# Block-sparse attention and a feed-forward net in one kernel: the first segment scored in fp32 from the raw rows, the mask built in five operations a part, weight lows that scale as they subtract, and new ranks in the planner

## The chip, the cores and the metric

The kernel runs on one core of one Trainium2 chip. The metric is the device time of one execution in microseconds, the median of several runs. Profiles come from one execution each; all times in a profile are counted from the first instruction.

## The reference

```python
# attention: B, H, S, D = 4, 8, 768, 64; blocks of 32; scale = 1/8
scores = scale * q @ k.T
mask = |blk_i - blk_j| <= 1, or row or column block first or last, or blk_j in sampled_blocks[blk_i]  # 3 a row
scores = where(mask, scores, -1e9);  attn = softmax(scores);  a = attn @ v
# feed-forward on x = a laid out as (4, 768, 512)
xn = (x - mean) / sqrt(var + 1e-6) * g_ln
out = x + relu(xn @ w_ch1) @ w_ch2        # 512 -> 2048 -> 512
```

q, k and v come in fp32. The two weight matrices come in 64 bits a number, and the kernel makes fp32 of their bits itself.

## The kernel before

**Work.** A unit is one batch and 256 query rows: 12 units. A unit has four segments, one for each pair of heads, and a segment has two query tiles of 128 rows, so four slots (tile, head). A pair of heads shares one 128-row tile of q and k, each head in 64 of its rows. Precision comes from splitting: a number x is kept as a half-precision high part and the rest as a half-precision low part, and a product is three half-precision matmuls (high by high, high by low, low by high).

**A slot.** TensorE (PE) writes the scores of both heads of a tile (`scores`, line 518, "ps"); VectorE (DVE) adds the mask and takes the maximum in one custom operation (`masked_max`, line 527); ScalarE (ACT) takes the exponential with the sum (`exponent`, line 541). Then there are two ways. The first `EARLY` segments go the early way: PE transposes the fp32 probabilities (line 556), ACT copies them out of PSUM (line 563, "pt"), and PE multiplies them with v in fp32 (line 632) and spreads the sums (line 657). All others go the usual way: ACT and DVE write the scaled high and low (lines 593 and 597, "ph" and "pl"), the DMA queue transposes them, and PE multiplies in half precision (lines 636 and 641). Before a v tile of an early segment is used the usual way later, ACT scales it (line 373) and splits it.

**After a unit's four segments** come the layer norm and the feed-forward net. For the first `EARLYLN` units the mean and the variance are fp32 matmuls against ones (line 713), for the others DVE adds four parts to one first and PE needs two half-precision matmuls for each (lines 705 and 706). The first product, here "up", is 192 matmuls (line 800), whose bank ACT and DVE turn into `hh` and `hl` (lines 815 and 821), and the second, "down", is 192 matmuls (line 860 for unit 0, which takes the weight rows in order; line 881 for the others).

**Weights.** Eight parts of w1 (each 1 MB of raw bits) and 16 of w2 (0.5 MB) are loaded and converted while the first units run. DVE shifts and masks the bits in three operations (lines 465, 469, 473), ACT scales (line 500), ACT writes the high (line 502), and GpSimd (POOL), or for parts named in `LOWDVE` DVE, writes the low (line 504). For parts in `PORC` the third operation is a short one (line 478) and POOL adds (line 483), so that ACT has no scaling to do.

**Start.** The first k and q ("raw" and "qr") are loaded first; ACT casts the high of k (line 335), DVE the high of q (line 356), and DVE subtracts both lows (lines 362 and 330). `build_mask` then makes the mask of the first two tiles in eight DVE operations (lines 288 to 298), and that of the other four in as many, later.

**Order.** `Plan` holds every task with an engine, a cost, a rank and what it waits for; it plays the program through once and emits the tasks in the order that comes out. Each engine then works in that order and waits at each instruction for what it needs: a later one never overtakes. DMAs are issued by SP's queue in order as well. Ranks come from the tables (`W1AT`, `W2AT`, `KAT`, `MASKAT` and so on).

## Time and profile before

| | |
|---|---|
| median of three runs | 797.96 us (797.42 to 801.64) |
| the profiled execution | 798.02 us, of which its span is 796.2 us |
| PE busy | 768.0 us, 96% of the span |
| DVE, ACT, POOL busy | 610.5, 519.1, 156.2 us |
| granted TensorE clock | 1.00 |
| first scores, first up, first down matmul | 5.01, 80.66, 124.94 us |
| last matmul ends | 792.85 us |

The table says which engine is busy over the whole span, not what holds it up at a given time: the stages have to be taken apart. A bracket behind a row of the timeline gives how long that engine sat idle before it, and what released it.

### The profile page before, as it was taken

The page shows a single profiled execution, that of the slowest core. Times are in us where ns is not written, and L with a number is a line of the kernel's source. Part 1 is how long each engine was busy: PE and PEld are TensorE (multiplying, and loading weights), DVE is VectorE, ACT ScalarE, POOL GpSimd, SP SyncE. Part 2 cuts the span into 40 slices and gives each one's busy share as a digit, 9 for nine tenths or more (in the row PEclk, how much of TensorE's full clock was granted, in tenths as well). Part 3 has the DMA queues.
Part 4 walks back from the last instruction along what each step waited for, and adds up shares of the span by engine and source line. Part 5 has one row for each costly group of instructions (what it writes and reads, how often), then busy time and mean ns, then how long its engine had stood idle before and what let it go on. Part 6 is the DMA issues. An engine that isn't in the chain of part 4 may idle for free.

```text
span 796.2 us, 18337 instructions
## 1 busy us (share of the span) xinstructions
PE 768.0 (96%) x7208; PEld 588.2 (74%) x7208; DVE 610.5 (77%) x1193; ACT 519.1 (65%) x974; POOL 156.2 (20%) x171
## 2 busy tenths in 40 slices
PE   5879899999999999999999999999999999999998
PEld 2555567777877777877777877677777777788887
DVE  6999999978887887877887978778978789744020
ACT  5899988868776666677666766668767667613010
POOL 2564423342110112322211013231110100000000
PEclk9999999999999999999999999999999999999999
DMA  8653459998887779897978789799887886620000
GB/s 313 204 199 119 122 102 218 199 198 158 150 129 153 132 140 175 163 185 145 162 132 133 148 152 162 157 189 168 151 147 130 132 138 122 110 62 2 28 1 28
DMA packets 298342, 112.61 MB, mean 141 GB/s; under 512 B 266640, under 2 KB 290064, under 8 KB 298256
## 3 DMA queue, kind: packets, MB, share of 16 engines
q1 hardware_dynamic: 290192, 106.49, 66.2%
q0 software_dynamic: 7776, 4.85, 5.1%
q8 instruction: 57, 0.93, 0.5%
q14 instruction: 29, 0.24, 0.1%
q10 hardware_dynamic: 288, 0.10, 0.1%
HBM read 45.46 MB, written 6.29 MB: 65 GB/s over the span
## 4 chain that ended last, share of the span: by engine, by line
PE 85%; DVE 8%; ACT 3%; DMA 2%; issue 1%; SPq 0%; DVEq 0%
PE bank L800 29%; PE bank L881 27%; PE ps L518 11%; PE pa L636 7%; PE pa L641 3%; PE bank L860 3%; DVE p L527 2%; PE pa L632 2%; ACT p L541 1%; PE bank L556 1%; ACT pt L563 1%; DVE w2l L504 1%; DVE pl L597 1%; DMA pt<-pl 1%; DMA raw<-w 1%
## 5 line engine op out<-in xcount | busy, mean ns | idle before, releaser
L881 PE MATMUL bank<-hh,w2h 128*128 128x256 f16 x704 | 192.2, 273 | 0.0
L881 PE MATMUL bank<-hh,w2l 128*128 128x256 f16 x704 | 191.9, 273 | 0.0
L881 PE MATMUL bank<-hl,w2h 128*128 128x256 f16 x704 | 191.9, 273 | 0.0
L527 DVE CUSTOM_DVE_ANT_1 p<-ps,allow 128x768 f32<-128x768 f32 x192 | 178.2, 948 | 12.5 <-PE ps L518 12.2
L541 ACT ACTIVATE p<-p,st 128x768 f32<-128x768 f32 x192 | 178.1, 930 | 14.1 <-DVE st L527 14.0
L597 DVE SCALAR_TENSOR_TENSOR pl<-p,st,ph 128x768 f16<-128x768 f32 x164 | 167.0, 1036 | 24.2 <-DMA pt<-pl 22.3
L593 ACT ACTIVATE ph<-p,st 128x768 f16<-128x768 f32 x164 | 148.9, 928 | 43.8 <-DVE st L584 26.7
L800 PEld LDWEIGHTS <-w1h 128*128 128x128 f16 x1536 | 147.4, 98 | 30.5 <-issue 13.8
L881 PEld LDWEIGHTS <-w2h 128*128 128x128 f16 x1408 | 135.0, 98 | 24.1 <-issue 8.8
L800 PE MATMUL bank<-xh,w1h 128*128 128x256 f16 x768 | 115.4, 273 | 4.4 <-ACT pt L563 2.3
L815 ACT ACTIVATE hh<-bank 128x512 f16<-128x512 f32 x96 | 56.9, 592 | 91.2 <-PE bank L800 90.7
L800 PE MATMUL bank<-xl,w1h 128*128 128x256 f16 x768 | 115.4, 273 | 0.0
L800 PE MATMUL bank<-xh,w1l 128*128 128x256 f16 x768 | 115.3, 273 | 0.0
L821 DVE SCALAR_TENSOR_TENSOR hl<-bank,hh 128x512 f16<-128x512 f32 x96 | 66.0, 688 | 48.4 <-ACT hh L815 47.7
L636 PE MATMUL pa<-pt,vh 128*64 128x512 f16 x492 | 83.3, 383 | 0.0
L800 PEld LDWEIGHTS <-w1l 128*128 128x128 f16 x768 | 74.3, 98 | 11.0 <-issue 2.6
L518 PE MATMUL ps<-kh,qh 64*128 64x256 f16 (+1 forms) x384 | 69.1, 332 | 11.7 <-DVE st L527 6.7
L881 PEld LDWEIGHTS <-w2l 128*128 128x128 f16 x704 | 68.9, 98 | 8.0
L518 PEld LDWEIGHTS <-qh 64*128 64x128 f16 x768 | 31.9, 95 | 57.5 <-issue 28.9
L641 PE MATMUL pa<-pt,vl 128*64 128x256 f16 x492 | 67.9, 273 | 0.0
L518 PE MATMUL ps<-kl,qh 64*128 64x256 f16 (+1 forms) x384 | 66.9, 327 | 0.7 <-DVE kl L330 0.7
L518 PE MATMUL ps<-kh,ql 64*128 64x256 f16 (+1 forms) x384 | 65.8, 327 | 0.0
(114 smaller groups left out, 897.3 us busy)
## 6 DMA issues: line engine op xcount, KB each, us to landing
raw<-k SPq DMA_DIRECT2D x16, 384.0 KB, 4.8
qr<-q SPq DMA_DIRECT2D x48, 128.0 KB, 3.7
raw<-w SPq DMA_DIRECT2D x12, 512.0 KB, 4.4
out<-ot SPq DMA_DIRECT2D x48, 128.0 KB, 1.9
vr<-v SPq DMA_DIRECT2D x24, 192.0 KB, 2.9
w2l<-w SPq DMA_DIRECT2D x4, 1024.0 KB, 8.6
qh<-q POOLq DMA_DIRECT2D x44, 64.0 KB, 3.6
pt<-ph SPq DMA_TRANSPOSE x164, 2.8
```

The source lines that it names most:

```text
L518: nc.tensor.matmul(s.ps[:, lo:hi], x[rows, s.qs], y[rows, lo:hi], start=n == 0, stop=n == len(terms) - 1)
L527: nc.vector.tensor_tensor_reduce(out=s.p.rearrange(blk, k=BLK), in0=s.ps[:, 0:S].rearrange(blk, k=BLK), in1=bias, scale=-0.125, scalar=3.0 ...
L541: nc.scalar.activation(s.p, s.p, AF.Exp, bias=s.st[:, j : j + 1], scale=-1.0, accum_out=total)
L593: nc.scalar.activation(s.ph, s.p, AF.Copy, scale=s.r)
L597: nc.vector.scalar_tensor_tensor(out=s.pl, in0=s.p, scalar=s.r, in1=s.ph, op0=ALU.mult, op1=ALU.subtract)
L636: nc.tensor.matmul(seg.pa[half[hh], 0 : 2 * CH], vo.vh[:, hh, t, :], pts[keys[hh]][:, t].rearrange("p i n -> p (i n)"), start=t == 0, stop ...
L641: nc.tensor.matmul(seg.pa[half[hh], 0:CH], vo.vl[:, hh, t, :], pts[keys[hh]][:, t, 0, :], start=False, stop=t == KT - 1, skip_group_check= ...
L800: nc.tensor.matmul(dst, w[:, ct, fs], x[:, ct, :], start=n == 0 and ct == 0, stop=n == 2 and ct == CT - 1, skip_group_check=True)
L815: nc.scalar.activation(u.hh[:, f : f + 2, :].rearrange("p f n -> p (f n)"), bank[plan.where("bank", own)], AF.Relu)
L821: nc.vector.scalar_tensor_tensor(out=u.hl[:, f : f + 2, :].rearrange("p f n -> p (f n)"), in0=bank[plan.where("bank", own)], scalar=0.0, i ...
L860: nc.tensor.matmul(dst(e), w[:, f, e * P : (e + 1) * P], x[:, f, :], start=f == 0 and n == 0 and e % 2 == 0, stop=f == FT - 1 and n == 2, ...
L881: nc.tensor.matmul(dst, w[:, k, e * P : (e + 1) * P], x[:, k, :], start=k == 0 and n == 0, stop=k == FT - 1 and n == 2)
```

## The change

It has four parts and new numbers for the planner.

1. The first segment (`RAWS_S = 1`) is scored by one fp32 matmul a part from the raw k and q rows, in place of three half-precision ones. The high and the low of the first q are no longer made; those of the first k still are, since later units need them, its low now on POOL. The raw buffer of the first k comes free when both the low and the segment's last score are done.
2. `build_mask` compares all three sampled blocks at once, straight from the integers, and then takes three maxima and one affine operation.
3. Parts in `LOWDVE` and not in `PORC` skip ACT's scaling: ACT writes the high with the scale, and DVE writes the low as scale times source minus high in one operation.
4. `EARLY` goes from 7 to 8, so that all of units 0 and 1 go the early way, and `EARLYLN` from 2 to 1, so that unit 1's layer norm goes the usual way.
5. New tables; `LOWDVE` holds one part of w1 and eight of w2 (before: one and twelve), `PORC` two of w1 and five of w2 (before: one and five).

```diff
-    LOOK = 60
+    LOOK = 90
...
-    EARLY = 7
-    EARLYLN = 2
-    EASY, EASE = 34, (34, 1649, 802)
-    PORC = ((1, 6), (2, 1), (2, 5), (2, 12), (2, 15), (2, 0))
+    EARLY = 8
+    EARLYLN = 1
+    EASY, EASE = 50, (210, 1787, 613)
+    PORC = ((1, 6), (2, 1), (2, 5), (1, 0), (2, 4), (2, 14), (2, 0))
...
+    RAWS_S = 1
+    SPLITAT = -2.2
+    LOWDVE = ((2, 0), (2, 6), (2, 7), (2, 12), (2, 1), (2, 11), (2, 8), (1, 0), (2, 14))
...
-    W2AT = (15.45, 15.53, 15.97, 18.44, 18.44, 18.89, 21.76, ...
+    W2AT = (10.58, 12.15, 16.02, 16.59, 18.19, 19.41, 20.61, ...
...
-        nc.vector.tensor_copy(samp_f[:, ts],
-                              samp_i.rearrange("p c (r t) -> p c r t", t=2)[:, ts, :, 0])
...
+        hit = one[:, 0 : n * NR * NB].rearrange("p (t r n) -> p t r n", r=NR, n=NB)
+        ids = allow[:, KT : KT + 1, :].unsqueeze(1).to_broadcast([P, n, NR, NB])
+        got = samp_i.rearrange("p c (r t) -> p c r t", t=2)[:, ts, :, 0:1]
+        nc.vector.tensor_tensor(out=hit, in0=ids, in1=got.to_broadcast([P, n, NR, NB]),
+                                op=ALU.is_equal)
         for r in range(NR):
-            nc.vector.tensor_tensor(out=hit, in0=ids,
-                                    in1=samp_f[:, ts, r : r + 1].to_broadcast([P, n, NB]),
-                                    op=ALU.is_equal)
-            nc.vector.tensor_tensor(out=allow[:, ts], in0=allow[:, ts], in1=hit, op=ALU.max)
+            nc.vector.tensor_tensor(out=allow[:, ts], in0=allow[:, ts], in1=hit[:, :, r],
+                                    op=ALU.max)
...
+            d = c if own in LOWDVE else plan.add(
+                "ACT", 960 * size + 60, lambda: nc.scalar.activation(
+                    o.src, o.src, AF.Copy, scale=scale), (c,), rank)
+        left = scale if own in LOWDVE and own not in PORC else 1.0
...
+                nc.scalar.activation(o.dh, o.src, AF.Copy, scale=left)
...
+                nc.vector.scalar_tensor_tensor(out=o.dl, in0=o.src, scalar=left, in1=o.dh,
+                                               op0=ALU.mult, op1=ALU.subtract)
...
-        terms = (q.qh, k.kh), (q.qh, k.kl), (q.ql, k.kh)
+        terms = ((q.qr, k.kr),) if a.seg.i < RAWS_S else (
+            (q.qh, k.kh), (q.qh, k.kl), (q.ql, k.kh))
```

The order of the engines' queues shows what the new ranks do. First DVE at the start of the program, from its first instruction on data, before and then after the change ("w1h<-allow" and "allow" are the mask, "p,st<-ps,allow" the masked maximum, "w2h<-w1r" a weight part's bits, "w1l" a weight low).

```order
L356 CAST qh_132<-qr_133 128x256
L362 TENSOR_TENSOR ql_121<-qr_133,qh_132 128x256
L330 TENSOR_TENSOR kl_130<-raw_119,kh_129 128x768
...
L527 ISA p_190,st_191<-ps_169,allow 128x768
...
L527 ISA p_197,st_191<-ps_170,allow 128x768
...
L465 TENSOR_SCALAR w2h<-w1r_156 128x1024
L469 SCALAR_TENSOR_TENSOR w2h<-w1r_156,w2h 128x1024
L527 ISA p_224,st_225<-ps_203,allow 128x768
...
L473 SCALAR_TENSOR_TENSOR w2h<-w1r_156,w2h 128x1024
```

```order
L293 TENSOR_TENSOR w1h<-allow,samp_i 128x144
L296 TENSOR_TENSOR allow<-allow,w1h 128x48 x3
L298 TENSOR_SCALAR allow<-allow 128x48
L546 ISA p_176,st_177<-ps_152,allow 128x768
...
L546 ISA p_179,st_177<-ps_153,allow 128x768
...
L468 TENSOR_SCALAR w2h<-w1r_150 128x1024
L472 SCALAR_TENSOR_TENSOR w2h<-w1r_150,w2h 128x1024
L481 TENSOR_SCALAR w1r_150<-w1r_150 128x1024
L546 ISA p_203,st_204<-ps_186,allow 128x768
```

The three operations on q and k are gone from the head of the queue; behind the first two maxima all three bit operations of the first weight part now stand ahead of the next maximum, where before two did.

Then DVE around the end of unit 0's up product, where the last `hl` stands; line 716 and its neighbours are unit 1's layer norm, "xc" its centring, "raw" a w2 part's bits, "w2l" a w2 low. Before the change:

```order
L821 SCALAR_TENSOR_TENSOR hl_1075<-bank_102,hh_1068 128x512
L597 SCALAR_TENSOR_TENSOR pl_1470<-p_1307,st_1308,ph_1418 128x768
L597 SCALAR_TENSOR_TENSOR pl_1491<-p_1322,st_1308,ph_1438 128x768
L821 SCALAR_TENSOR_TENSOR hl_1075<-bank_103,hh_1068 128x512
L504 TENSOR_TENSOR w2l<-raw_120,w2h 128x512
L465 TENSOR_SCALAR raw_119<-raw_119 128x512
```

And after it:

```order
L840 SCALAR_TENSOR_TENSOR hl_1023<-bank_101,hh_1010 128x512
L472 SCALAR_TENSOR_TENSOR raw_118<-raw_118 128x512
L476 SCALAR_TENSOR_TENSOR raw_118<-raw_118 128x512
L750 TENSOR_TENSOR xc_1585<-xT_802,bank_101 128x256 x2
L518 SCALAR_TENSOR_TENSOR w2l<-raw_118,w2h 128x512
L750 TENSOR_TENSOR xc_1585<-xT_802,bank_101 128x256
L468 TENSOR_SCALAR raw_119<-raw_119 128x512
```

Unit 1's layer norm and the last weight parts now follow the last `hl` at once, with no attention between them; unit 1's four segments are finished before unit 0's down product starts. On PE that product's 192 matmuls begin with 160 among which only the four matmuls of the layer norm stand, where before they were mixed with four pairs of heads' scores and two products with v.

## The prediction

> **What bounds the kernel now.** I read the busy time by stage first, cutting the span where the first up matmul starts (80.66), where unit 0's down product starts (124.90) and behind the last matmul. Columns: stretch, its length, busy time of PE, its weight loads, DVE, ACT and POOL (instructions), granted clock, DMA share, GB/s.

> ```profile
> 0.00:15.00 15.00, 5.69 (x28) 2.76 (x29) 9.82 (x21) 5.51 (x9) 3.59 (x9) 1.00 0.82 285
> 15.00:80.66 65.66, 55.19 (x448) 35.27 (x447) 61.63 (x112) 62.25 (x129) 34.69 (x25) 1.00 0.58 191
> 80.66:124.90 44.24, 40.09 (x348) 28.58 (x348) 42.32 (x81) 38.08 (x77) 15.45 (x17) 1.00 0.54 121
> 124.90:792.80 667.90, 667.02 (x6386) 521.62 (x6385) 496.33 (x981) 413.27 (x761) 102.49 (x120) 1.00 0.75 135
> 792.80:796.20 3.40, 0.05 (x1) 0.00 (x0) 0.42 (x1) 0.00 (x0) 0.00 (x0) 1.00 0.11 39
> ```

> From 124.90 on PE idles 0.88 us in 667.90: there the time is PE's work and nothing on another engine can shorten it. All of PE's other idle time is 9.31 us in the first stage, 10.47 in the second, 4.15 in the third and 3.35 behind the last matmul, where the last output is stored. So the time is PE's work plus its idle time, and the change can win at most what lies ahead of 124.90. In the second stage ACT is busy for 62.25 of 65.66 us and in the third DVE for 42.32 of 44.24. I read next who PE waited for there: the first four rows are the second stage, the two behind them the longest of the third (a wait of 1.6 us ends just at the cut and is in both answers; I count it in the second).

> ```profile
> PE bank L556 <- ACT pt L563: 5.8, 8, 1.4
> PE ps L518 <- DVE st L527: 2.2, 3, 1.6
> PE bank L800 <- ACT pt L563: 1.6, 1, 1.6
> PE bank L556 <- ACT p L541: 0.8, 2, 0.4
> ```

> ```profile
> PE bank L800 <- ACT pt L563: 2.3, 2, 1.6
> PE bank L800 <- DVE hl L821: 2.2, 2, 1.6
> ```

> ACT's copies and exponentials end 8.2 of the 10.4 us in the second stage; in the third DVE's `hl` and ACT's copies share the rest. A microsecond taken from ACT's queue ahead of the first up matmul is therefore worth about one; one taken from DVE there is worth little, since ACT would stay behind.

> **The start: fp32 scores and the shorter mask.** The timeline of the first 19 us: ACT's queue issuing the allowed blocks and their time to landing, then DVE's rows, POOL's, ACT's and PE's:

> ```profile
> 1.18 0.46 ACTq L262 DMA_DIRECT2D allow<-blocks  x1
> ```

> ```profile
> allow<-blocks ACTq DMA_DIRECT2D x1, 84.0 KB, 3.6
> ```

> ```profile
> 4.64 0.29 DVE L356 CAST qh<-qr 128x256 f16<-128x256 f32 x1 [3.49 <-DMA qr<-q]
> 5.31 0.95 DVE L330 TENSOR_TENSOR kl<-raw,kh 128x768 f16<-128x768 f32 x1
> 6.62 0.21 DVE L297 TENSOR_TENSOR allow<-allow,w1h 128x48 f32<-128x48 f32 x1
> 6.86 1.55 DVE L294 TENSOR_TENSOR w1h<-allow,samp_f 128x48 f32<-128x48 f32 x1
> 8.45 0.59 DVE L297 TENSOR_TENSOR allow<-allow,w1h 128x48 f32<-128x48 f32 x1
> 10.28 0.96 DVE L527 CUSTOM_DVE_ANT_1 p<-ps,allow 128x768 f32<-128x768 f32 x1
> 12.52 0.69 DVE L465 TENSOR_SCALAR w2h<-w1r 128x1024 int32<-128x1024 int32 x1 [0.40 <-DMA w1r<-w]
> 14.39 0.95 DVE L527 CUSTOM_DVE_ANT_1 p<-ps,allow 128x768 f32<-128x768 f32 x1
> ```

> ```profile
> 6.72 1.64 POOL L330 TENSOR_TENSOR kl<-raw,kh 128x768 f16<-128x768 f32 x1 [5.40 <-ACT kh L335]
> ```

> ```profile
> 4.13 0.83 ACT L335 CAST kh<-raw 128x768 f16<-128x768 f32 x1 [1.18 <-DMA raw<-k]
> 15.34 0.59 ACT L563 COPY pt<-bank 128x512 f32<-128x512 f32 x1 [2.11 <-PE bank L556]
> ```

> ```profile
> 11.30 0.58 PE L518 MATMUL ps<-kh,qh 64*128 64x512 f16 x1 [3.31 <-DVE st L527]
> 13.41 0.42 PE L518 MATMUL ps<-kh,qh 64*128 64x256 f16 x1
> 13.63 0.42 PE L518 MATMUL ps<-kl,qh 64*128 64x256 f16 x1
> 14.19 2.82 PE L556 MATMUL bank<-ident,p 128*128 128x128 f32 x12
> ```

> Taken at face value the change starts the first scores at 4.64, when q has landed, and empties DVE's queue of what it does from 4.64 to 6.26 on q and k, and of three mask operations. But two things stand behind it. The first is POOL: the mask operation at 6.86 took 1.55 us where the same took 0.21, until POOL's subtraction from 6.72 ended at 8.36, and the next took 0.59; what DVE does on two tiles waits while POOL subtracts. After the change POOL has the first k's low as well, from 4.96, when ACT's cast ends, and then the second's from 6.7 as now, and two of q. The allowed blocks land at 1.18 + 3.6 = 4.8, so one mask operation runs free and four go one by one into the gaps between POOL's: behind the first k's low (6.7), the second's (8.4) and those of q (0.6 each, like the row at 8.45). The mask is ready at 9.1 to 9.7, and the first maximum starts there, not at 10.28; I take 9.7.

> The second is the DMA queue. The next maximum stands behind the first weight part's operations, and that part landed at 12.5; nothing that is ahead of it in the queue is taken away, though it is issued one place earlier, which may bring 0.5 us. Two bit operations fill 12.52 to 14.39 now; a third, a short one like the first, adds 0.6, so the third maximum starts at 14.5 to 15.0, against 14.39. Nothing of the start's gain is left on this queue but about 1 us of work done beforehand.

> On PE a half-precision pass over 256 columns takes 0.22 us here (13.41 to 13.63), and 0.11 later (below). No row shows an fp32 matmul in half the rows; fp32 in half the columns is the nearest (below), at four passes for both heads together, so 768 columns cost 4 x 3 x 0.22 = 2.6 us against 2.0 for the three terms. Were the two heads not side by side it would be 5.2, the upper bound. The second pair then starts when the first maximum has read its bank, at 10.6 instead of 11.3, and ends at about 14.2 as now. So ACT's unbroken work starts at 15.3 as before: I cost the start at nothing (-1.2 to +1.5).

> [...]

> **ACT's queue up to the first up matmul.** In the two orders ACT's instructions ahead of the first `xh` cast differ by three: one scaling of a w1 part (part 0 goes by POOL's adding) and two scalings of v, which now come later. Their rows, that of a w2 scaling, and one of the second mask on DVE (columns: count, busy us, mean ns, idle before):

> ```profile
> L500 ACT ACTIVATE w2h<-w2h 128x1024 f32<-128x1024 f32 x7 | 7.4, 1061 | 1.0 <-DVE w2h L473 1.0
> L373 ACT ACTIVATE vr<-vh 128x384 f32<-128x384 f32 x4 | 2.1, 526 | 0.4 <-POOL vl L381 0.4
> L500 ACT ACTIVATE raw<-raw 128x512 f32<-128x512 f32 x5 | 3.1, 627 | 1.0 <-DVE raw L473 1.0
> ```

> ```profile
> L297 DVE TENSOR_TENSOR allow<-allow,w1h 128x96 f32<-128x96 f32 x3 | 3.0, 989 | 0.1
> ```

> An instruction overlaps the next by some 0.09 (DVE's first bit operation and its third maximum show the same), so they free 0.97 + 2 x 0.44 = 1.9 us. ACT also idled 3.4 us in this stage (65.66 - 62.25), of which 1.0 is behind DVE's bits. DVE loses much there: half of the second mask's operations (its maxima took 0.99 us each, held up by POOL) and the work done beforehand. I take that 1.0 and a little more, 1.2 of the 3.4. Together -3.1: the first up matmul at 77.5. Bounds: -1.9 - 3.4 = -5.3 if ACT never waits, and 0 if the two moved operations and POOL's larger load (it adds for w1 part 0, and ACT's cast and then DVE's new low wait for that ahead of the fifth maximum) eat all.

> **Between first up and first down.** PE has more to do here than before: 7 pairs of scores in place of 5 and segment 7's early products. ACT loses five w2 scalings over this stage and the next (0.54 each, 2.7 us), DVE four w2 lows to POOL and segment 7's `pl`. So there is more for PE to turn to, and less on the two engines it waits for. I take half of the 4.15 us of idle time away, -2.1. Bounds: all of it, -4.15; and +2 if DVE's `hl`, which PE's banks wait for, stand behind POOL more often, since POOL gets four more lows.

> **PE's own work.** Segment 7 early instead of usual, and unit 1's two statistics:

> ```profile
> 26.09 2.74 PE pa L632 x24
> 31.08 0.87 PE L556 MATMUL bank<-ident,p 128*128 128x128 f32 x6
> 310.21 0.41 PE L636 MATMUL pa<-pt,vh 128*64 128x512 f16 x2
> 311.86 0.38 PE L636 MATMUL pa<-pt,vh 128*64 128x512 f16 x2
> 41.56 0.60 PE L713 MATMUL bank<-xT,ones 128*128 128x256 f32 x2
> 301.18 0.27 PE L518 MATMUL ps<-kh,ql 64*128 64x256 f16 x2
> 301.39 0.61 PE L800 MATMUL bank<-xl,w1h 128*128 128x256 f16 x4
> 301.83 0.60 PE L800 MATMUL bank<-xh,w1h 128*128 128x256 f16 x4
> ```

> Early: 24 transposes at 0.11 (0.87 less a tail of 0.2, over six) are 2.7, the product 2.7, the spread 0.4: 5.8. Usual: six steps of 0.33 (310.21 to 311.86 are five): 2.0. Plus 3.8. The statistics: 16 fp32 passes of 0.21 (two in 0.60 with a tail of 0.17) against four half-precision ones of 0.11, -3.0. Seven changes fewer between scores, whole-tile and half-tile matmuls, each 0.1 (301.18 to 301.39 less one pass): -0.6. Net +0.2; the fp32 scores' 0.6 lie in the start. Bounds +-1.

> **After the first down matmul.** PE's down product takes a w2 part's 12 matmuls in 1.3 us (four in 0.44 above), and 160 of 192 now stand in one run, so it reaches part 15 some 22 us on instead of 30 (160 at 0.11, 3 for a product and a pair, 20 more). DVE's queue has 25 instructions between the last `hl` and the third operation on part 15, at 0.3 to 1 us some 14 us in all; ACT's scaling and cast (0.54 each) and POOL's low add some 3: ready at about 17. Nothing waits, with 5 us to spare. I add 0.1 for the stage: 0 to +4.

> **Sum.** Start 0, ACT's queue -3.1, up to the first down -2.1, PE's work +0.2, later +0.1: -4.9, a span of 791.3. With the 1.8 us that lie around the span (798.02 - 796.2) it is 793.1; I say 793.2. The profiled execution stands 0.06 above the median of the runs, so no shift between them.

> **The rivals.**
> - *ACT's queue is freed of its 1.9 us, but all waits stay*: what is left waits for PE's transposes or DVE as now. 798.0 - 1.9 + 0.2 = 796.3. For it: PE's order up to the first up matmul is nearly the same, and ACT idles for it too (the 2.11 at 15.34). Chance 0.24.
> - *All the waits go*: -5.3, -4.15, +0.2 and up to 1 us from the start: 788 to 791, say 790. For it: DVE sheds work on q, k, the masks, w2 lows and segment 7. Against: POOL's holds and ACT's order. Chance 0.19.
> - *PE reaches its full rate ahead of the second pair's twelve transposes*, which then take 0.11 and not 0.23 each, 1.4 us less before ACT can begin: 793.2 - 1.4 = 791.8. The rows at 14.19 speak against. [...] Chance 0.05.
> - *Slower: the down product runs out of weight rows.* The last four w2 parts take turns in two buffers, and a load starts only when the low that frees its buffer is written; their issues stand on SP's queue behind segment 8's transposes. If part 15's low comes later than 22 us after the first down matmul, each microsecond is one of PE's. It takes 10 us of lateness to lose the 4.9 gained, and some 14 to be 4 us slower, 802, as when three loads in turn come 5 us late each. The estimate above leaves 5 to spare. Chance 0.09.
> - My forecast, 791.5 to 795: 0.43.

> **From these the numbers.** A change of 0.5%, 4 us, is about what can be told from none here. Of the forecast's 0.43 some 0.29 lies below 794, with the second and third rivals 0.53; slower by as much is 0.06 of the fourth's 0.09; 0.41 is left for no change. The range runs from 789.2, inside the second rival, to 798.8, past the first: it leaves out a part of the second and most of the fourth, less than 0.2.

> **What would show it.** In the new profile: the first maximum at 9 to 10, not at 7; the third at 14.5 to 15.0 behind the landing of the first weight part; ACT busy without a gap from about 15.3; the first up matmul at 77.5 (75.3 to 80.7); PE's idle time between it and the first down matmul near 2; PE idle under 1 us after that, at parts 12 to 15 above all. I am wrong if the mask's operations run free of POOL and the weight part lands by 10 (faster), or if PE waits for a w2 low in the down product (slower).

## The result, and the profile after

The kernel after takes 802.7 us (median of 22 runs, 800.4 to 807.2 but for one disturbed execution) against 798.6 for the kernel before (22 runs beside it): a ratio of 1.0050, 95% interval 1.0036 to 1.0064. The forecast was 793.2, so it is 9.5 us off and on the wrong side. The profiled execution took 800.4 us, 2.3 below the median and the fastest of the 22; its span is 798.5.

The busy time of the kernel after in the stages that the prediction used, cut at its own first up matmul (82.05), first down matmul (127.28) and last matmul:

```profile
0.00:15.00 15.00, 8.98 (x29) 4.91 (x30) 8.26 (x18) 6.93 (x13) 6.17 (x11) 1.00 0.89 304
15.00:82.05 67.05, 55.71 (x440) 35.17 (x440) 62.49 (x102) 58.18 (x121) 38.45 (x26) 0.95 0.54 179
82.05:127.28 45.23, 44.90 (x420) 33.13 (x420) 43.48 (x85) 41.49 (x89) 21.62 (x22) 1.00 0.52 123
127.28:795.14 667.86, 663.69 (x6334) 520.51 (x6331) 494.74 (x977) 410.40 (x751) 102.84 (x120) 1.00 0.69 133
```

Two rows tell the story. The second stage has become longer (67.05 us, before 65.66) though ACT has 4.1 us less to do in it, and PE's clock was granted at 0.95 only. And the last stage takes 667.86 us, as before (667.90), though 52 matmul records (6386 to 6334) and, by the counts of instructions at their durations, about 6 us of PE's work have moved ahead of it (in a run below that has no waits there, the same 6334 matmuls take 660.96 us). The third stage is the success: PE idles 0.33 us there (45.23 - 44.90) and not 4.15, with more work done.

What PE waited for, in the second stage and behind the first down matmul (us in total, times, longest):

```profile
PE ps L537 <- DVE st L546: 4.0, 5, 2.7
PE bank L575 <- ACT p L560: 3.9, 4, 1.7
PE bank L575 <- ACT pt L582: 3.0, 4, 1.4
```

```profile
PE ps L537 <- DVE st L546: 3.0, 6, 0.6
PE bank L819 <- DVE hl L840: 1.0, 1, 1.0
```

Ahead of the first up matmul ACT still ends 6.9 us of the waits (before 8.2), but VectorE's maxima (`st`) now end 4.0, before 2.2; and behind the first down matmul PE waits 3.0 us for maxima, before 0.8. The timelines of VectorE and of POOL in the kernel after show the first of these:

```profile
26.11 2.53 DVE L476 SCALAR_TENSOR_TENSOR w2h<-w2l,w2h 128x1024 int32<-128x1024 int32 x1
28.71 0.42 DVE L683 TENSOR_TENSOR xT<-pa,xT 128x256 f32<-128x256 f32 x1
29.06 0.45 DVE L293 TENSOR_TENSOR w1h<-allow,samp_i 128x288 f32<-128x288 f32 x1
29.54 3.36 DVE L296 TENSOR_TENSOR allow<-allow,w1h 128x96 f32<-128x96 f32 x3
32.94 0.21 DVE L298 TENSOR_SCALAR allow<-allow 128x96 f32<-128x96 f32 x1
33.06 0.95 DVE L546 CUSTOM_DVE_ANT_1 p<-ps,allow 128x768 f32<-128x768 f32 x1
```

```profile
23.93 3.62 POOL L330 TENSOR_TENSOR kl<-raw,kh 128x768 f16<-128x768 f32 x2 [6.79 <-ACT kh L337]
29.13 2.37 POOL L516 TENSOR_TENSOR w1l<-w2h,w1h 128x1024 f16<-128x1024 f32 x1
31.45 1.33 POOL L365 TENSOR_TENSOR ql<-qr,qh 128x256 f16<-128x256 f32 x2
```

The three maxima of the second mask (line 296) need 0.28 us each when POOL is idle (below); here the last of them ends 0.1 us behind POOL's subtractions (31.45 + 1.33 = 32.78). The whole mask takes 4.1 us (29.06 to 33.15). In the kernel before its eight operations stood at 26.00 to 30.69 and took 4.7:

```profile
26.00 0.14 DVE L288 CAST samp_f<-samp_i 128x12 f32<-128x12 int32 x1
27.05 2.10 DVE L297 TENSOR_TENSOR allow<-allow,w1h 128x96 f32<-128x96 f32 x1
30.48 0.21 DVE L298 TENSOR_SCALAR allow<-allow 128x96 f32<-128x96 f32 x1
```

Three operations fewer have saved 0.6 us, since both masks last about as long as POOL's subtractions beside them. The scores that wait for the maxima behind the mask, and the clock in the next 7 us:

```profile
34.07 0.58 PE L537 MATMUL ps<-kh,qh 64*128 64x512 f16 x1 [2.74 <-DVE st L546]
34.00:41.00 7.00, 6.63 (x30) 3.21 (x31) 5.87 (x10) 3.93 (x7) 3.33 (x3) 0.51 0.12 25
```

The second finding is on the page of each kernel, in the group of the low parts (`pl`); idle time and its releaser stand at the end, the kernel before first:

```profile
L597 DVE SCALAR_TENSOR_TENSOR pl<-p,st,ph 128x768 f16<-128x768 f32 x164 | 167.0, 1036 | 24.2 <-DMA pt<-pl 22.3
```

```profile
L616 DVE SCALAR_TENSOR_TENSOR pl<-p,st,ph 128x768 f16<-128x768 f32 x160 | 168.2, 1059 | 41.3 <-DMA pt<-pl 39.9
```

VectorE stands 39.9 us, before 22.3, until a transpose has read one of the two `pl` buffers. In the chain that ended last DMA's share went from 2% to 10%. From 156 to 186 us SP's queue issues one transpose after the other, with a few loads and stores between them:

```profile
170.70 1.25 SPq L622 DMA_TRANSPOSE pt<-ph  x1
172.04 1.25 SPq L625 DMA_TRANSPOSE pt<-pl  x1
173.39 1.23 SPq L622 DMA_TRANSPOSE pt<-ph  x1
```

That is one every 1.34 us where nothing stands between, and by 155 us 12 of unit 2's 32 were out, where the kernel before had 16.

### The profile page after: what moved, and what is told of

Its sections match the earlier page's. It is cut to its first block, busy times and chain, and to the rows that moved or that the text cites. A ratio compares the mean times of both kernels' runs of the same rounds, so it can differ in the third digit from the quotient of the medians.

```text
span 798.5 us, 18337 instructions
## 1 busy us (share of the span) xinstructions
PE 773.3 (97%) x7220; PEld 593.7 (74%) x7220; DVE 609.4 (76%) x1180; ACT 517.0 (65%) x971; POOL 169.1 (21%) x177
## 4 chain that ended last, share of the span: by engine, by line
PE 70%; DVE 13%; DMA 10%; ACT 5%; issue 2%; SPq 0%; DVEq 0%; ACTq 0%
PE bank L900 24%; PE bank L819 23%; PE ps L537 9%; DMA pt<-pl 7%; PE pa L655 5%; DVE pl L616 4%; DVE p L546 3%; PE bank L879 3%; PE pa L660 2%; PE pa L651 2%; DMA pt<-ph 2%; ACT p L560 2%; DVE hl L840 1%; PE bank L575 1%; DMA w1r<-w 1%
## 5 line engine op out<-in xcount | busy, mean ns | idle before, releaser
L616 DVE SCALAR_TENSOR_TENSOR pl<-p,st,ph 128x768 f16<-128x768 f32 x160 | 168.2, 1059 | 41.3 <-DMA pt<-pl 39.9
L612 ACT ACTIVATE ph<-p,st 128x768 f16<-128x768 f32 x160 | 145.4, 929 | 67.1 <-DVE st L603 36.3
L655 PE MATMUL pa<-pt,vh 128*64 128x512 f16 x480 | 81.5, 383 | 0.0
L537 PE MATMUL ps<-kh,qh 64*128 64x512 f16 (+1 forms) x376 | 69.0, 329 | 7.0 <-DVE st L546 7.0
L537 PE MATMUL ps<-kl,qh 64*128 64x512 f16 (+1 forms) x376 | 66.3, 325 | 0.0
L365 POOL TENSOR_TENSOR ql<-qr,qh 128x256 f16<-128x256 f32 x47 | 39.1, 834 | 123.0 <-DMA qr<-q 70.5
```

The costliest lines, as they stand in the source:

```text
L365: o.low = plan.add("POOL", 660, lambda: nc.gpsimd.tensor_sub(o.ql, o.qr, o.qh), (o.raw, o.high), rank, give=(("qr", n),), lock=True)
L537: nc.tensor.matmul(s.ps[:, lo:hi], x[rows, s.qs], y[rows, lo:hi], start=n == 0, stop=n == len(terms) - 1)
L612: nc.scalar.activation(s.ph, s.p, AF.Copy, scale=s.r)
L616: nc.vector.scalar_tensor_tensor(out=s.pl, in0=s.p, scalar=s.r, in1=s.ph, op0=ALU.mult, op1=ALU.subtract)
L655: nc.tensor.matmul(seg.pa[half[hh], 0 : 2 * CH], vo.vh[:, hh, t, :], pts[keys[hh]][:, t].rearrange("p i n -> p (i n)"), start=t == 0, stop ...
```

## The experiments

Each kernel ran in five rounds beside the kernel before; ratios are to that. The runs lie on five chips, so a difference in us to the kernel after is one between medians of different chips, and the ratios are the safer measure (the kernel after stands at 1.0050). Stage times are of each one's profiled execution. "All queues kept" means that the planner's order was not played anew.

### Which part of the start was lost

**The operations in the old order.** The kernel before, with the new mask, the fp32 scores and `if own in LOWDVE` no scaling by ACT:

```diff
-            d = plan.add("ACT", 960 * size + 60, lambda: nc.scalar.activation(
+            d = plan.add("ACT", 960 * size + 60, lambda: own in LOWDVE or nc.scalar.activation(
...
-        terms = (q.qh, k.kh), (q.qh, k.kl), (q.ql, k.kh)
+        terms = ((q.qr, k.kr),) if a.seg.i == 0 else (
+            (q.qh, k.kh), (q.qh, k.kl), (q.ql, k.kh))
```

> The kernel before, with its order of all queues kept, and only the operations of the change put in: the first segment scored in fp32 from raw rows (which lie in a place that no weight part needs yet), the mask in five operations a part, the first k's low on POOL, and nine w2 parts without ACT's scaling. EARLY, EARLYLN and all ranks stay as before. Theory A (the operations are a gain, and it was the new order that lost it): the first maximum about 2 us earlier, ACT freed of 4.8 us, first up matmul at 78 to 80 (before 80.66, after 82.05), clock 1.00, run 795 to 797.5 against 798.6. Rival (the operations themselves bring the collisions of DVE and POOL that the new trace shows at 26 to 42 us): first up at 81 or later, granted clock below 1.00 somewhere in 25 to 45, run 799 or more.

Measured: 799.05, ratio 1.0014 (1.0003 to 1.0025); first up at 80.98. The first maximum came at 9.69, as forecast, held by POOL. This is near to the rival: first up 0.02 us short of its 81, the granted clock at 0.50 from 23.7 to 27.1, the run slower by a trifle. ACT has 0.4 us less to do in the second stage and idles 0.7 more, and 3.1 less in the third and idles 2.5 more: most of what it no longer has to do in the old order it waits for. What the operations alone would be worth at the full clock, which the kernel before had all through in its profiled execution, this run doesn't show.

**The second mask cut short.**

```diff
-        for r in range(NR):
+        for r in range(NR if lo == 0 else 0):
```

> The kernel after, the order of all queues kept; the second mask leaves the sampled blocks out (one operation in place of five), so VectorE is rid of the 0.45 us of L293 and the 3.36 us of the three L296 at 29.1 to 32.9. Theory B (the start was lost since VectorE stood on POOL there, so that PE had nothing for 2.74 us and its clock fell to 0.50 from 34 to 40.6): the idle time ahead of the scores at 34.07 shrinks from 2.74 to under 0.7, the granted clock stays 1.00, the first up matmul comes at 76.5 to 79 instead of 82.05, and the run is 2 to 5 us faster than the kernel after (802.7): 797.5 to 800.5. Rival (POOL holds whatever VectorE does next, and the mask's own time is hidden): first up moves less than 1.5 us, clock still falls, run 801.5 to 803.

Measured: 798.55, 1.0007 (0.9993 to 1.0022), 4.1 us faster than after by the medians, 3.4 by the ratios; first up at 79.2, 0.2 past the range. Theory B, but for the clock: it stayed at 1.00 from 34 to 41 and fell for 3.4 us at 44.8.

**The gap filled.**

```diff
+        if a.i == 10:
+            filler(..., 22)   # 22 matmuls into a free bank, ahead of these scores
```

> The kernel after, the order of all queues kept, with 22 extra half-precision matmuls of 256 columns (0.11 us each, their result unused) on PE ahead of the scores that start at 34.07, that is in the idle 2.74 us. VectorE and POOL do what they did. Theory B1 (the gap alone lets the clock fall): granted clock 1.00 all through 34 to 41, scores, statistics and products there at full rate, first up 2 to 3.5 us earlier (78.5 to 80), run 799 to 801 against 802.7. Rival B2 (the clock falls for the sparse work since 17 us, or VectorE's holds alone set the pace, so that the rate does not matter): clock still falls, or it does not and first up moves less than 1 us; run 802 to 803.5.

Measured: 804.39, 1.0082 (1.0065 to 1.0100). The clock held where it had fallen:

```profile
32.56 2.56 PE L282 MATMUL bank<-ones,ones_h 128*128 128x256 f16 x22
34.00:41.00 7.00, 6.15 (x55) 3.95 (x54) 6.10 (x14) 4.14 (x8) 3.25 (x3) 1.00 0.33 107
```

PE got through 55 matmul records there in place of 30, and the first up matmul came at 80.66, 1.4 us earlier than after and 2.5 earlier than in two runs below (no low transposes, no wait for statistics) that start alike and have half the clock for 6.8 us there: 83.20 and 83.14. So the low rate is a part of what the start lost, less than B1 and more than B2 had it. The run was still no faster than after (1.0050): the second down product (the expectations call its start D1) began at 185.64, as after (185.70), and 671.79 us lie behind its first down matmul. What was won ahead was lost again there.

**The mask moved.** Its five operations are emitted behind the second maximum:

```diff
-             plan.add("DVE", 1300, lambda: build_mask(TS, KT), (), MASKAT, 100, lock=True)]
+             plan.add("DVE", 1300, lambda: None, (), MASKAT, 100, lock=True)]
...
+        if s.i == 1:
+            build_mask(TS, KT)
```

> The kernel after with one move: the five operations of the second mask stand on VectorE's queue right behind the second maximum, at 9.5 us, where VectorE idles 1.9 us for the first weight part, and not at 29 to 33. All other places are kept. Theory B (VectorE held by POOL at 29 to 33 is what the start lost): the mask takes 1.5 to 2.5 us of the idle 1.9 and of the next row, the third maximum moves by less than 0.7, first up at 78.5 to 80 (82.05 after, 79.2 with the mask cut short), run 798 to 800.2. Rival (POOL's two subtractions for q from 9.0 to 10.3 hold it here too, and the third maximum and all of ACT's work behind it start 1.5 us later): first up 80.5 or later, run 800.5 to 803.

Measured: 798.16, 0.9998 (0.9981 to 1.0015), 4.5 us faster than after; first up at 77.93. VectorE's timeline:

```profile
10.66 0.45 DVE L293 TENSOR_TENSOR w1h<-allow,samp_i 128x288 f32<-128x288 f32 x1
11.15 0.84 DVE L296 TENSOR_TENSOR allow<-allow,w1h 128x96 f32<-128x96 f32 x3
12.03 0.21 DVE L298 TENSOR_SCALAR allow<-allow 128x96 f32<-128x96 f32 x1
14.69 0.95 DVE L546 CUSTOM_DVE_ANT_1 p<-ps,allow 128x768 f32<-128x768 f32 x1
```

Theory B. With POOL idle the same mask takes 1.6 us in place of 4.1, in time in which VectorE waited for the first weight part. Three kernels below have the same order up to the first up matmul, and it comes at 77.66 (second queue), 78.62 (four buffers) and 81.39 (one pair forward) in theirs. The stage up to there, in the first and the last of these:

```profile
15.00:77.66 62.66, 53.36 (x445) 34.31 (x443) 57.42 (x99) 58.91 (x124) 38.96 (x26) 1.00 0.58 194
15.00:81.39 66.39, 57.40 (x452) 36.35 (x451) 59.61 (x100) 59.40 (x124) 37.70 (x26) 0.92 0.56 184
```

The clock was never low in the first and stood at 0.50 for 10.2 us in the last, whose first maximum came 0.8 us later (9.70, 8.92). So the clock can move the end of this stage by some 2.9 us from one execution to the next (81.39 - 77.66 - 0.8), an estimate from these two.

But 669.9 us lie behind this kernel's first down matmul, 2 more than in the kernel after: half of what the start gained is lost again there.

### What is lost behind the first down matmul

**Fewer bit operations.** `second` and `third` return at once for w2 parts from 10 on.

> The kernel after, the order of all queues kept, without the second and third bit operation (0.69 us each) on w2 parts 10 to 15 (the one short third operation of part 14 stays), 7.5 us of VectorE's work, nearly all of it between 100 and 152 us. What is open: behind the first down matmul (127.3) the kernel after takes as long as the kernel before (667.9) though 6 us of PE's work stand ahead of that point now; its waits there are 3.2 us longer, most of all for scores behind maxima at 160 to 170. Theory D (VectorE, busy for 50.5 of 52 us from 100 to 152, does the weights late and with them unit 2's attention, and PE's lead is lost waiting for it): idle time of PE from 150 to 200 falls from 1.6 to under 0.4, the run is 2 to 5 us faster than after (802.7): 797.5 to 800.5. Rival (the transposes on SP's queue, one every 1.33 us from 156 to 186, or the planner's places for PE's tasks set the pace): idle stays over 1, run within 1 us of after, 801.5 to 803.5.

Measured: 804.29, 1.0067 (1.0052 to 1.0083). Theory D falls: VectorE had 13.3 us to do from 127 to 145 and not 17.8, yet the same number of transposes was out by 155, and the second down product began at 186.07 (185.70 after), though its first down matmul had come 1.2 us later (128.48).

**No wait for statistics.**

```diff
-                                     bank[plan.where("bank", mb)][:, 0:CH])
+                                     o.s if i == 1 else bank[plan.where("bank", mb)][:, 0:CH])
```

and the same for the logarithm.

> The kernel after, the order of all queues kept; unit 1's centring and logarithm read the sums that VectorE made (no mean over the partitions), so that VectorE and ACT no longer wait for PE's two statistics matmuls, which stay. Theory G (unit 1's statistics, which go the usual way only since the change, are a chain PE to VectorE to ACT to VectorE to PE to ACT from 126 to 142, and unit 2's exponentials and highs stand behind it on ACT, which idles 7.9 us there, so that only 2 transposes are issued from 130 to 145 against 8 before): ACT's wait of 3.6 us at 137 to 141 goes, 13 or 14 of unit 2's transposes are out by 155 instead of 12, D1 at 184 to 185.3 instead of 186.0, run 1 to 3 us faster than after: 799.7 to 801.7. Rival (the exponentials wait for scores and maxima whose places PE's and VectorE's order sets, the chain only fills the time): transposes by 155 still 12, run 802 to 803.5.

Measured: 801.92, 1.0052 (1.0029 to 1.0075): as after. The transposes by 155 were still 12 (its first down matmul came at 128.37, 1.1 later). Theory G falls.

**One pair forward.** By hand, two lows, a reciprocal, two highs and their transposes ahead of unit 1's centring, on the kernel with the mask moved (the numbers are those of tasks):

```diff
+    AHEAD = {450: [1114, 1116], 455: [1118, 1120], 949: [1095, 1097, 1099, 1101, 1112, 1113, 1115, 1117, 1119]}
+    BEHIND = {952: [436, 437, 438, 439, 441, 447]}
```

> The kernel with the second mask at 9.5 us (798.2 at its run), and one pair of unit 2's attention moved forward by hand: the two lows of slots 34 and 35, whose highs are ready at 126, the reciprocal and the highs of slots 36 and 37, whose exponentials are ready at 127, with their four transposes, stand on VectorE, ACT and SP ahead of unit 1's centring (some 2.3 us of VectorE, while it waits for the mean) and not behind its logarithm; one w2 part's operations go behind the centring for it. Nothing else is moved. Theory F1 (the transposes start late because of this order): 16 of unit 2's transposes or more are out by 155 instead of 14, PE's idle time at 150 to 200 falls from 2.8 to under 1.2, D1 2 to 3.5 us earlier, and the run 1.5 to 4 us faster than with the mask moved alone: 794.2 to 796.7, which would be faster than before. Rival F2 (SP's queue or the DMA engines are the pace of unit 2 whatever starts first, or the delayed w2 part holds the down product): within 1 us of 798.2.

Measured: 802.12, 1.0039 (1.0026 to 1.0052), by the ratios 3.3 us slower than with the mask moved alone. In the profiled executions the first down matmul already comes 3.5 us later (126.70, 123.16), where the order is the same and the clock was low for longer (above); behind it 670.50 us against 669.94. By 135 us 10 transposes were out in place of 6, but by 155 only 12 in place of 14: unit 1's layer norm came late instead, and PE stood still for it in the down product, where it had never waited:

```profile
PE bank L741 <- ACT vah L728: 2.0, 1, 2.0
```

F1 in this form falls: nothing was won behind the first down matmul. From 100 to 152 VectorE has no time to give in the kernel after (50.5 of 52 us busy).

**No low transposes, in both kernels.**

```diff
-                nc.sync.dma_start_transpose(out=pts[key][:, :, 1, s.qs], in_=s.pl)
...
-                                             pts[keys[hh]][:, t].rearrange("p i n -> p (i n)"),
+                                             pts[keys[hh]][:, t, 0:1].to_broadcast([P, 2, CH]),
```

> The kernel after, the order of all queues kept, without the transposes of the low parts (pl) of the usual segments; the products read the high part twice, so PE's work is the same. SP's queue and the DMA engines have 160 transposes of 1.33 us less to do. Theory F (unit 2's attention starts late, and from 156 to 186 the transposes follow each other on SP's queue without a gap, so that neither an earlier PE, as in the run with the filled gap, nor a freer VectorE, as in the run with fewer bit operations, brings the second down matmul ahead of 186): the down product of unit 1 starts at 182.5 to 184.5 instead of 186.0, unit 2's up product at 213 to 215.5 instead of 217.6, and the run is 3 to 6 us faster than after (802.7): 796.7 to 799.7. Rival (PE's, VectorE's and ACT's queues hold each other, with the transposes only along): D1 within 1 us of 186, run 801.5 to 803.5.

> The same edit on the kernel before: no transposes of the low parts, the high part read twice. Theory F: in the kernel before 16 of unit 2's 32 transposes are out by 155 us (12 in the kernel after), PE idles 0.9 us behind the first down matmul, so there is next to nothing to win: 797.3 to 799, that is within 0.1% of before, and with the run above the kernel after then stands level with before or ahead. Rival (the transposes take something from every stage, by the DMA engines' load or by holding back the outputs and loads on SP's queue): 2 us faster or more, 796.5 or less.

Measured: after 793.89, 0.9944 (0.9932 to 0.9956), 8.8 us less than the kernel after; before 796.99, 0.9984 (0.9973 to 0.9995), 1.3 us less. From the first down matmul to the last:

```profile
128.55:789.53 660.98, 660.96 (x6334) 518.47 (x6331) 496.16 (x977) 409.54 (x751) 105.71 (x120) 1.00 0.41 87
```

```profile
124.73:792.72 667.99, 667.08 (x6388) 521.61 (x6385) 500.90 (x981) 413.03 (x761) 104.08 (x120) 1.00 0.45 88
```

Without these transposes the kernel after (the first row) has no waits at all there, and is 6.9 us shorter; the kernel before (the second) is not shorter at all. Theory F, and in the kernel after more than it asked, though the second down product began at 184.74, just past its range; the kernel before came out 0.3 us below its range and 0.5 above the rival's.

**Only unit 2 without them.** The same edit under `s.u.i == 2`.

> The kernel after (mask where the change put it) without the low transposes of unit 2 alone (16 of 160; its products read the high part twice). Theory F1 (unit 2's late start is the loss, and what is lost later follows from it): D1 at 184.5 to 185.3 and unit 2's up product at 215 to 216, as in the run without any low transposes, and at least 3.5 of the 8.8 us are won: 797 to 799.2. Rival F3 (each unit loses some to the transposes, since the planner's allowances are too small everywhere): only 1.5 to 2.5 us are won, 800.2 to 801.2.

Measured: 799.75, 1.0008 (0.9995 to 1.0021): 2.9 us by the medians, 3.4 by the ratios; second down product at 183.56. Unit 2 is somewhat under half of the loss, the rest is spread over later units: between F1 and F3. The last stage is 3.3 us shorter than after (664.60).

**A second queue.** The lows of every second head of unit 2 issued by ACT (`nc.scalar.dma_start_transpose`).

> The kernel with the second mask at 9.5 us, and 8 of unit 2's 32 transposes (the lows of the second head of each pair) issued from ACT's queue in place of SP's. The DMA engines have the same to do. Theory F2a (SP's queue is the pace: one issue every 1.33 us): unit 2's last transposes leave 8 to 10 us earlier than SP could send them, PE's idle time at 150 to 200 falls under 1.2, run 795 to 797 in spite of ACT's issues (1.2 us each, in time that it idles). Rival F2b (the DMA engines, 0.95 busy at 150 to 200, are the pace, or ACT's issues hold exponentials and highs back): no gain, 798 to 802.

Measured: 822.37, 1.0307 (1.0285 to 1.0330). A failure by far more than either theory had. SP's waits show why:

```profile
SPq L624 <- DMA pt<-pl: 37.5, 8, 7.5
```

A transpose on SP's queue now waited until one on ACT's had landed. So this run does not tell whether SP's issues or the engines set the pace.

**Four buffers.** Highs and lows take turns in four buffers instead of two; order and operations are those of the kernel with the mask moved:

```diff
-                s.pl = pp.tile([P, S], F16, tag="pl", name=f"pl{s.i}")
+                if s.i < 40 or s.i // 2 % 2:
+                    s.pl = pp.tile([P, S], F16, tag="pl", name=f"pl{s.i}")
+                else:
+                    at = S + s.i % 2 * (S // 2)
+                    s.pl = raw_s[0][:, at : at + S // 2].bitcast(F16)
```

and the same for `ph` in `raw_s[1]`.

> The kernel with the second mask at 9.5 us, order and operations unchanged, and from slot 40 on the highs and lows take turns in four buffers each in place of two (the two new ones lie in the second halves of the two raw buffers, which no weight part uses any more). Theory H (a late transpose reaches PE through VectorE's queue: the low part waits for its buffer, the maxima stand behind it, and PE's scores wait for the maxima): VectorE's waits for pt<-pl from 150 to 260 fall from 17.2 us to under 4, PE's idle time behind 150 from 6.1 us to under 2.5, and the run is 2 to 4.5 us faster than with the mask moved alone (798.2): 793.7 to 796.2, faster than both kernels. Rival (the transposes' pace on SP's queue is itself the bound of unit 2, so PE's products wait for pt instead of the scores for maxima): PE's idle time as before, now at the products, run 797.2 to 799.

> The same four buffers (from slot 48 on) in the kernel before. Theory H: PE idles 0.9 us there behind the first down matmul, so nothing is to be won: 797.5 to 799, within 0.1% of before. Rival (the buffers hold every version back): 796.5 or less.

> The kernel after exactly as it is (second mask at 29 us), with the four buffers for highs and lows from slot 40 on. Theory H (what was lost behind the first down matmul, 5.8 us more than in the kernel before, came through the two buffers): from the first down matmul to the last 661.5 to 663.5 us in place of 667.9, run 4.5 to 6.5 us faster than after: 796.2 to 798.2, a little faster than before. Rival (the buffers only matter when the start is earlier, as with the mask moved): run 799.5 to 802.

Measured: with the mask moved 792.49, 0.9935 (0.9922 to 0.9948), faster than both kernels; the kernel before with four buffers 796.64, 0.9983 (0.9974 to 0.9992); the kernel after with four buffers and nothing else 796.40, 0.9962 (0.9944 to 0.9979), 6.3 us faster than after by the medians. The last stage of the first and of the last of these:

```profile
123.88:786.61 662.73, 661.63 (x6334) 520.25 (x6331) 495.73 (x977) 409.03 (x751) 105.68 (x120) 1.00 0.70 134
```

```profile
128.26:791.42 663.16, 661.55 (x6334) 518.87 (x6331) 495.96 (x977) 408.93 (x751) 102.96 (x120) 1.00 0.71 134
```

The transposes are as many and as long as before, and the stage is 4.7 us shorter than in the kernel after (667.86), 7.2 shorter than with the mask moved alone (669.94): theory H. In the kernel before the buffers won a little too: 796.64 is below the 797.5 that theory H had as its least, though not at the rival's 796.5, and its last stage went from 667.90 to 666.78. On the page of the kernel with both edits VectorE's lows are two groups, the first written into the old buffers, the second into the new ones; idle time ahead of them and what ended most of it stand at the end:

```profile
L626 DVE SCALAR_TENSOR_TENSOR pl<-p,st,ph 128x768 f16<-128x768 f32 x84 | 89.3, 1075 | 1.4 <-ACT ph L618 1.3
L626 DVE SCALAR_TENSOR_TENSOR raw<-p,st,raw 128x768 f16<-128x768 f32 x76 | 79.7, 1061 | 0.7 <-DMA pt<-pl 0.4
```

VectorE idles 2.1 us ahead of its lows, where it waited 39.9 us for transposes in the kernel after. ACT's highs waited 19.2 us for theirs there and have no such wait with four buffers; since both had their buffers doubled, the share of each isn't told apart.

The path was not from the transposes to PE's products (PE's weight loads waited 0.4 us for them in the kernel after), but from the transposes to the buffers, from there to the queues of VectorE and ACT, and, in VectorE's, from the maxima that stand behind the low to PE's scores.

### The planner's numbers one by one

Four kernels put one number or two back and let the planner play the order anew.

```diff
-    EASY, EASE = 50, (210, 1787, 613)
+    EASY, EASE = 34, (210, 1787, 613)
```

> The kernel after with one number of the planner back: tasks of unit 2 (ranks 34 to 49) are again planned with the large allowances for late data (EASY 34 instead of 50, EASE unchanged). All queues stay as they are until past the first up matmul. Theory C (behind the first down matmul PE waits since unit 2's attention is planned without slack): first up unchanged at 82, PE's idle time between 127 and 260 falls from 2.2 to under 0.7, run 1 to 3 us faster than the kernel after: 799.7 to 801.7. Rival (unit 2's attention is simply late, at the pace of VectorE and of the queue of transposes, wherever PE's tasks stand): idle time and run stay within 1 us of after (802.7).

```diff
-    EARLY = 8
-    EARLYLN = 1
+    EARLY = 7
+    EARLYLN = 2
```

> The kernel after with segment 7 the usual way and unit 1's statistics by fp32 matmuls again (EARLY 7, EARLYLN 2); all other numbers new. The queues are as they are in the kernel after until shortly before the first up matmul. Theory E (the part of the change that moved segment 7 and the statistics took PE's work forward but VectorE's additions and ACT's scalings of v backward, into the stage that has no slack): first up about 82, and run 2 to 5 us faster than after: 797.5 to 800.5. Rival (the new ranks were made for EARLY 8, what is lost is lost in the weights' order): run the same as after or slower, 802 to 808.

> The kernel after with only unit 1's statistics by fp32 matmuls again (EARLYLN 2), EARLY 8. Per count of instructions PE has 3.0 us more to do and VectorE ten operations less. Theory E (the usual way of the statistics is what delays unit 1's up product and unit 2's attention): run 1 to 4 us faster than after in spite of PE's 3.0 us: 798.7 to 801.7. Rival (it only adds PE's work where PE is the bound): 804 to 807.

```diff
-    EASY, EASE = 50, (210, 1787, 613)
+    EASY, EASE = 50, (210, 1649, 802)
```

> The kernel after with the planner's allowances for late data of all units behind unit 2 as before (EASE (210, 1649, 802) instead of (210, 1787, 613); EASY stays 50). The queues are as in the kernel after for units 0 and most of 1. Theory C2 (in units 3 to 11 tasks of VectorE and ACT are planned with 0.19 us less allowance, so PE waits there): PE's idle time from 190 to 560 falls from 2.4 to under 1.2 and the run is 1 to 3 us faster, 799.7 to 801.7. Rival (these waits come from what was lost before 190, or from the places of the transposes): 802 to 804.

Measured: 809.31 (1.0144, 1.0124 to 1.0163), 809.32 (1.0136, 1.0116 to 1.0155), 819.41 (1.0261, 1.0241 to 1.0282) and 803.31 (1.0062, 1.0046 to 1.0079). None is faster than after, and theories C and E fall as they were put. But they say little more: each number moves hundreds of instructions on all queues, so what comes out is another order and not the same one with one thing changed. The runs above that kept the order are the ones that settle the cause.

## Why the prediction was wrong

Step by step, against the profiled executions.

- **Start, 0 (-1.2 to +1.5): held.** The first maximum came at 7.67 in the profiled execution of the kernel after, since POOL paused between its subtractions, but at 9.3 to 9.8 in twelve of the fifteen kernels made from it and at 8.9 in three: the 9.7 of the forecast is the usual case. The third maximum came at 13.89 there and at 13.4 to 15.4 in the others, forecast 14.5 to 15.0.
- **ACT's queue up to the first up matmul, -3.1: this step failed.** The first up matmul came at 82.05, 1.4 us later than before and not 3.1 earlier. The term that was wrong is the 1.2 us taken for "half of the second mask's operations" (three of eight went, not half), and with it the rule that VectorE's time is worth little there since ACT would stay behind. I counted operations, though I had just read from the first mask that an operation lasts until POOL ends. The second mask's new place is beside two of POOL's subtractions, and it takes 4.1 us there, nearly the old 4.7; with a freer ACT nothing hid it, and it stood ahead of the maxima, so that PE stood for 2.74 us. PE's clock then fell to 0.50 for 6.8 us, which the prediction didn't count on at all; with the gap filled the first up matmul came 1.4 us earlier. In a place where POOL rests the mask takes 1.6, and the first up matmul comes at 77.93: the forecast of 77.5 was near for a kernel with that mask elsewhere, in executions in which the clock stayed high.
- **Between first up and first down, -2.1: right in kind, too small.** Idle time fell from 4.15 to 0.33, so -3.8.
- **PE's own work, +0.2: held.** By counts of instructions at their durations it is +0.7, within the bounds of 1.
- **After the first down matmul, +0.1 (0 to +4): this step failed too, and it is the larger one.** The stage should have become shorter by the work that moved ahead of it, and did not. I asked only whether w2 rows would be late, the fourth rival; they were not (PE idles 0.03 us from the first down matmul to 160). I did not ask whether unit 2's attention would be ready when PE came to it 5.0 us sooner (unit 1's up product at 151.94, before 156.96). It was not: fewer of its transposes had begun, and two buffers then turned late transposes into late maxima: the waits in this stage went from 0.9 us to 6.9 (667.86 less the 660.96 of the same matmuls without waits). Four buffers take 4.7 us off the stage with the kernel otherwise unchanged.

So the forecast stood in three steps of five. With what failed in the other two changed, by moving the mask and adding buffers, the kernel takes 792.5, and the forecast was 793.2; that the two numbers are so near is partly luck, since the middle stage won more than forecast. On the rivals: the down product did not run out of weights; that ACT's 1.9 us are freed and the waits stay did not happen either, since the first up matmul came later and not sooner; that PE would be at its full rate ahead of the second pair's twelve transposes happened in part in some executions: these took 2.23 us in the profiled one, 2.41 with the mask moved, and 2.82, as in the kernel before, in five others. What stays open: why the transposes follow each other every 1.34 us, the queue's issues or the engines; and how much of the 2.3 us between the profiled execution and the median comes from the start, where an execution with the first maximum at 9.7 and a clock that falls for 6.8 us at 35 has its first up matmul at about 83 (83.24 in the run with fewer bit operations), and how much from the last stage.

## What to carry to other kernels

Fewer operations on an engine that is held by another one save little (0.6 us for three of eight here): ask where the operation stands and what runs beside it, and move it before shortening it. When a change lets the bounding engine arrive earlier at a later stage, go through everything that stage needs, the in-order queues and the number of their buffers above all; a wait for a buffer in one queue holds back whatever stands behind it (here 39.9 us of waits ahead of VectorE's lows, and 3.0 us of PE's for maxima in the last stage). And test a scheduled kernel with edits that keep its order, since a number put back in the planner makes another kernel.

## What the runs showed of the hardware

```profile
17.15 0.61 PE L540 MATMUL ps<-kh,qh 64*128 64x512 f16 x2
17.55 0.64 PE L540 MATMUL ps<-kl,qh 64*128 64x512 f16 x2
...
18.36 0.27 PE L540 MATMUL ps<-kh,qh 64*128 64x256 f16 x2
18.48 0.27 PE L540 MATMUL ps<-kl,qh 64*128 64x256 f16 x2
```

  The same scores in the kernel after, where 64x512 takes 0.23 us:

```profile
14.91 0.37 PE L537 MATMUL ps<-kh,qh 64*128 64x512 f16 x1 [0.25 <-DVE st L546]
...
15.79 0.58 PE L537 MATMUL ps<-kl,qh 64*128 64x512 f16 x2
16.02 0.57 PE L537 MATMUL ps<-kh,ql 64*128 64x512 f16 x2
```

  What starts such a step no run shows.
- **Some operations of VectorE that met a subtraction of POOL's ended only behind it:** 2.53 us for line 476 against 1.20 alone, and 4.04 for line 472 against 1.23, in the kernel after. The first ended 1.09 us behind POOL's subtractions (28.64, 27.55), and POOL's next one then took 1.08 us where 0.68 is usual, so each held the other up. The masked maximum was not held: it took 0.95 at 24.35 and at 25.23, inside POOL's subtractions from 23.93 to 27.55. So the prediction's "what DVE does on two tiles waits while POOL subtracts" is right for the mask's operations that it read it from, and too wide for all.
- **A transpose on SP's queue waited until one on ACT's had landed, in this program:** 37.5 us in 8 waits, the longest 7.5, in the run with a second queue; whether the chip would let them overlap no run shows.
